# Attention with pooled keys and a gated layer on one core: exponentials by head from PSUM, and the order of POOL and w_out work

## Chip, cores and metric

The kernel runs on one core of one Trainium2 chip. The metric is the device time of one execution in microseconds (us). The kernel before took 963.73 us (median of 3 runs, 963.48 to 965.11).

## The reference

There are 8 batches of 8 heads, 576 positions and 64 numbers per head. Keys and values are averaged over groups of 8 positions, which leaves 72 of each. The attention result, 4608 rows of 512, goes through a gated layer with a hidden width of 1536.

```python
k_p = k.reshape(B, H, Sp, 8, D).mean(axis=3)
v_p = v.reshape(B, H, Sp, 8, D).mean(axis=3)
scores = scale * np.matmul(q, k_p.transpose(0, 1, 3, 2))
scores = scores - np.max(scores, axis=-1, keepdims=True)
attn = np.exp(scores)
attn = attn / (np.sum(attn, axis=-1, keepdims=True) + 1e-09)
x = np.matmul(attn, v_p)          # as rows: 4608 x 512
g = x @ w_gate
out = (g / (1.0 + np.exp(-g)) * (x @ w_val)) @ w_out
```

Each factor of the large products is carried as two 16-bit parts, a high and a low one, so one product of the reference is three matmuls.

## The kernel before, in words

**Tiles, pieces, steps.** The 4608 rows are cut into 9 tiles of 512. A tile is made of 4 or 5 *pieces* of up to 128 rows of one batch, 40 in all. `answer` takes a piece through the attention: scores on PE into two PSUM banks of four heads each (L578), `less_max` on DVE (per bank a maximum, L587, and a subtraction that also moves the scores to SBUF, L588), the exponent of all eight heads in one ACT instruction (L595 or L599), the row sums on DVE (L605 or L616), one or two small operations on the eight sums (L610 or L617) and their reciprocal (L611, L621). ACT and POOL then make the high and the low 16-bit part (L649, L654), a DMA transposes them, PE multiplies by the values (L678, L679), and DVE divides (L683). The first two batches (`b < SPLIT`, 10 pieces, called old) take an older route that normalises before the product (L625).

Each tile then takes 12 *steps*, one for each 128 columns of the hidden width. A *plain* step is 24 matmuls of 512 columns (`plain_step`, L775 to L777). A *fast* step saves a product: 7 products of 6 matmuls of 256 columns (`fast_step`, L879), between which ACT copies partial sums (L937, L939, L946) and DVE adds them (L942, L947). A fast step needs sums of the weights (`fast_weights`: DVE L800, POOL L806 and L819, ACT L812) and of the tile (`fast_x`: L840, L844, L845, L848), so a step is fast only from the time on when both stand. Tile 0 has 16 steps, some of half width; there are 112 steps, each with a tanh on ACT (L723) and two operations on DVE (L726, L731). The results go to memory, and the last stage, after the last step, multiplies them by w_out (L1586, L1600, L1601, operands from L1483, L1487, L1497).

**Beside the steps.** Batches 2 to 7 need pooled sums of keys and values: `kv_part` loads a sixth at a time and adds on POOL (L1169 to L1171). `out_weights` decodes the 64-bit w_out in 12 chunks, on DVE and ACT, and writes it back to memory.

**What sets the order.** `Order` (L64) writes the instructions of all engines in one order while the program is built. It keeps a planned time for each engine, takes the operation that could start first by its table of durations, and by rank among those that are close. Lines wait for flags (`yield flag(...)`), for buffers from pools (`get`, `put`), and a flag that is raised later moves work later. `tile_steps` makes a step fast when the weights' sums are planned to stand soon, and plain otherwise. On the chip every engine then works in this fixed order.

Of the kernel before, what the change touches and what calls it, by code (L numbers as in the profile page):

```python
# [9 lines left out]
F32 = mybir.dt.float32  # L10
# [4 lines left out]
ALU = mybir.AluOpType  # L15
# [48 lines left out]
class Order:  # L64
# [37 lines left out]
    def get(self, name):  # L102
        return "get", name

    def flag(self, name):
        return "flag", name
# [85 lines left out]
def attention_then_swiglu(  # L192
# [71 lines left out]
    nc.gpsimd.memset(shares[:, 1:2], 1.0 / POOLW)  # L264
    least = const.tile([P, 4], F32, name="least")
    nc.gpsimd.memset(least, 1e-30)
    logunit = const.tile([P, 1], F32, name="logunit")
    nc.gpsimd.memset(logunit, LOGUNIT)

    spare = early.tile([P, 2 * NJ * SP + 6 * NJ * P // 2], F32, name="spare", tag="early")  # L270
    ksum = [
# [306 lines left out]
                nc.tensor.matmul(o, qt[rows, j, :n], keys[rows, j], start=True, stop=True)  # L578
        return pss

    def less_max(b, n, pss, sc=None, groups=(0, 1)):
        sc = sc or buffer(at, [P, H, SP], F32, "sc")
        mx = small.tile([P, 2, GH], F32, name="mx")
        heads = "p (j g) s -> p g j s"
        for g in groups:
            pv = pss[g][:n, : GH * SP].rearrange("p (h s) -> p h s", h=GH)
            nc.vector.tensor_reduce(out=mx[:n, g], in_=pv, axis=AX.X, op=ALU.max)  # L587
            nc.vector.tensor_tensor(  # L588
                out=sc[:n].rearrange(heads, g=2)[:, g], in0=pv,
                in1=mx[:n, g].unsqueeze(2).broadcast_to([n, GH, SP]), op=ALU.subtract,  # L590
            )
        return sc

    def exponentials(n, sc):
        nc.scalar.activation(sc[:n], sc[:n], AF.Exp, scale=EXPSCALE)  # L595

    def weights(b, n, sc):

        nc.scalar.activation(  # L599
            sc[:n], sc[:n], AF.Exp, bias=logunit[:n], scale=EXPSCALE  # L600
        )

    def row_sums(n, sc):
        sm = small.tile([P, H], F32, name="sm")
        nc.vector.tensor_reduce(out=sm[:n], in_=sc[:n], axis=AX.X, op=ALU.add)  # L605
        return sm

    def one_over(n, sm):
        ri = small.tile([P, H], F32, name="ri", bufs=4)
        nc.vector.tensor_scalar_add(sm[:n], sm[:n], 1e-9 * UNIT)  # L610
        nc.vector.reciprocal(ri[:n], sm[:n])  # L611
        return ri

    def inverse_sums(n, sc):
        sm = small.tile([P, H], F32, name="sm")
        nc.vector.tensor_reduce(out=sm[:n], in_=sc[:n], axis=AX.X, op=ALU.add)  # L616
        nc.vector.tensor_scalar(  # L617
            out=sm[:n], in0=sm[:n], scalar1=1e-9, scalar2=1.0 / UNIT, op0=ALU.add, op1=ALU.mult
        )
        ri = small.tile([P, H], F32, name="ri", bufs=4)  # L620
        nc.vector.reciprocal(ri[:n], sm[:n])  # L621
        return ri

# [76 lines left out]
    def scales(bs, mt):  # L700

        top = p2s[:, bs[0], 2:3]
        if len(bs) > 1:
            top = small.tile([P, 1], F32, name="top")
            nc.vector.tensor_max(top, p2s[:, bs[0], 2:3], p2s[:, bs[1], 2:3])
        nc.vector.tensor_mul(mt[:, :2], shares, top.broadcast_to([P, 2]))
        nc.vector.tensor_mul(mt[:, 2:3], mt[:, 0:1], mt[:, 1:2])
        rm = small.tile([P, 1], F32, name="rm")
        nc.vector.reciprocal(rm, top)
        ratios = {}  # L710
        for old in (True, False):
            some = [b for b in bs if (b < SPLIT) == old]
            if not some:
                continue
            r = small.tile([P, len(some)], F32, name=f"r{len(some)}", bufs=8)
            nc.vector.tensor_mul(r, p2s[:, some[0] : some[-1] + 1, 2], rm.broadcast_to([P, len(some)]))
            if old:
                nc.vector.tensor_single_scalar(r, r, 1.0 / UNIT, ALU.mult)
            ratios |= {b: r[:, n : n + 1] for n, b in enumerate(some)}
        return ratios  # L720

# [413 lines left out]
    def out_weights():  # L1135

        yield flag("decoded")
        for c in range(NCH):
            n, t0 = yield get("mid")
            tag, tf = yield get("wf")  # L1140
            wf = const.tile([P, DM], F32, name="wf1", tag=tag, bufs=1)
            _, t1 = yield get("load")
            t = yield bulk(512, lambda: o_load(c, n, wf), t0, t1)
            o = "out", c
            th = yield op("DVE", 330, lambda: w_shift(o), t)
            ts = yield op("ACT", 1260, lambda: w_sign(o), th)
# [30 lines left out]
    def prep(b):  # L1177

        split = yield flag("boxes")
        if b > SPLIT + 1:  # L1180
            split = yield flag(("split", b - 2))
        box(0)
        box(1)
        t = 0
        for c in range(6):
            order.start(("kv", b + 0.1 * c), kv_part(b, c, split))
        for c in range(6):
            t = max(t, (yield flag(("kv", b, c))))
# [54 lines left out]
    def answer(t):  # L1243
# [17 lines left out]
            t0 = max(t0, t1)  # L1261
        tp = yield op("PE", 1200 if t["n"] < 12 else 900, lambda: ps.update(scores(b, s0, m, homes)), ta, t0)
        put("qt", t["qt"], tp)
        for g in range(2):
            tm = yield op("DVE", 910, lambda: less_max(b, m, ps, sc, (g,)), tp, ts)
            put("att", homes[g], tm)
        tp = tm
        order.done(("scored", t["n"]), tp)
        if old:
            tp = yield op("ACT", 690, lambda: exponentials(m, sc), tp)  # L1270

            def sums_inv():
                t["ri"] = inverse_sums(m, sc)

            tp = yield op("DVE", 1300, sums_inv, tp)
            if t["n"] in ON_POOL:
                tp = yield op("POOL", 1300, lambda: normalise(nc.gpsimd, m, sc, t["ri"]), tp)
            else:
                tp = yield op("DVE", 750, lambda: normalise(nc.vector, m, sc, t["ri"]), tp)
            h, th = yield get("half")  # L1280
            half = halves[h]
            tp = yield op("ACT", 910, lambda: soft_high(m, sc, half), tp, th)
            tp = yield op("POOL", 1950, lambda: soft_low(m, sc, half), tp)
            put("sc", s, tp)
        else:
            te = tp = yield op("ACT", 865, lambda: weights(b, m, sc), tp)
            h, th = yield get("half")
            half = halves[h]
            tp = yield op("ACT", 665, lambda: blocks_high(m, sc, half), tp, th)
            tp = yield op("POOL", 1500, lambda: blocks_low(m, sc, half), tp)  # L1290
# [6 lines left out]
        r = rate[i][b]  # L1297
        if not old:

            def ratios():  # L1300
                sm = row_sums(m, sc)
                t["ri"] = one_over(m, sm)

            te = max(tr, (yield op("DVE", 1200, ratios, te)))
        where, t0 = yield get("wv" if old else "att")
        ps = {}
        x = xs[i]
# [378 lines left out]
    def all_lines():  # L1686
# [28 lines left out]
        for b in range(SPLIT, B):  # L1715
            left_of["b", b] = 0
        for n, (i, *sub) in enumerate(ahead):
            t = {"n": n, "at": (i, *sub)}
            left_of["b", sub[1]] = left_of.get(("b", sub[1]), 0) + 1
            if i < 2:  # L1720
# [82 lines left out]
```

## Time and profile before

| | |
|---|---|
| median of three runs | 963.73 us |
| the profiled execution | 958.7 us |
| its span, first to last instruction | 956.9 us |
| PE, DVE, ACT, POOL busy | 895.9, 717.6, 468.9, 580.4 us |
| mean granted clock of PE | 0.982 of full speed |

All rows below come from the profiled execution. Its time lies 1.8 us over its span and 5.0 us under the median. PE's busy time is modelled: matmuls are pipelined, and a matmul that is shown with 0.38 us can start every 0.22 us.

### The profile page before, as it was taken

The numbers are of one execution on the slowest core, as the hardware profiler recorded it, in microseconds if no ns is written. First come the engines' busy times: TensorE is split into PE (matmuls) and PEld (weight loads), VectorE is DVE, ScalarE is ACT, GpSimd is POOL, SyncE is SP. The second block draws the span as 40 slices with busy tenths as digits, with TensorE's granted clock in tenths as the row PEclk, the third lists the DMA queues.
The fourth block names the chain that finished last, engine by engine and source line by source line (L and its number), as shares of the span: only waits on it lengthen the run. The fifth ranks groups of instructions, "written<-read, shape, count | busy, mean of one in ns | idle before, by whom it ended". The sixth has DMA issues, their size and how long they took to land. (4 is left out here: it accounts for less than half of the span.)

```text
span 956.9 us, 17399 instructions
## 1 busy us (share of the span) xinstructions
PE 895.9 (94%) x6636; PEld 629.2 (66%) x6658; DVE 717.6 (75%) x1087; ACT 468.9 (49%) x809; POOL 580.4 (61%) x502
## 2 busy tenths in 40 slices
PE   5788898998989889999999999999899899999998
PEld 5775354444656667888888888888655455555554
DVE  7889898698877798688877645467737769496781
ACT  5578553334245455566664544355624344444442
POOL 3534998989988898454523404022646578678692
PEclk9799899999999999999999999999999999999999
DMA  9947857848748556557572421135560440806301
GB/s 342 289 123 245 264 149 188 227 117 210 187 127 220 171 116 165 151 116 173 136 161 81 97 72 57 56 108 196 195 217 23 164 188 21 309 23 241 111 23 66
DMA packets 134419, 146.53 MB, mean 153 GB/s; under 512 B 81600, under 2 KB 102080, under 8 KB 132032
## 3 DMA queue, kind: packets, MB, share of 16 engines
q1 hardware_dynamic: 134336, 145.42, 51.7%
q8 instruction: 52, 0.85, 0.4%
q14 instruction: 31, 0.25, 0.1%
HBM read 86.51 MB, written 40.89 MB: 133 GB/s over the span
## 5 line engine op out<-in xcount | busy, mean ns | idle before, releaser
L1600 PE MATMUL ps<-low,wsh 128*128 128x512 bf16 x384 | 146.2, 381 | 5.7 <-DVE low L1487 4.1
L879 PEld LDWEIGHTS <-mixed 128*128 128x128 f16 x1332 | 129.2, 98 | 23.4 <-issue 5.6
L879 PEld LDWEIGHTS <-wgv_h 128*128 128x128 f16 x1184 | 114.3, 98 | 33.2 <-issue 15.1
L723 ACT ACTIVATE hf<-ps,un 128x512 f32<-128x512 f32 (+1 forms) x112 | 74.8, 669 | 102.7 <-PE ps L879 62.3
L879 PE MATMUL ps<-xc,mixed 128*128 128x256 f16 x888 | 118.2, 274 | 3.5 <-ACT ps L939 3.5
L726 DVE SCALAR_TENSOR_TENSOR hf<-hf,ps 128x512 f32<-128x512 f32 (+1 forms) x112 | 74.1, 663 | 57.4 <-ACT hf L723 57.0
L879 PE MATMUL ps<-xc,wgv_h 128*128 128x256 f16 x592 | 104.8, 273 | 9.3 <-DVE ps L947 7.7
L777 PE MATMUL ps<-x,wgv_l 128*128 128x512 f16 (+1 forms) x304 | 110.5, 364 | 2.6 <-DVE wgv_l L389 2.6
L775 PE MATMUL ps<-x,wgv_h 128*128 128x512 f16 (+1 forms) x304 | 110.7, 364 | 0.4 <-ACT wgv_h L384 0.4
L776 PE MATMUL ps<-x,wgv_h 128*128 128x512 f16 (+1 forms) x304 | 110.6, 364 | 0.0
L731 DVE SCALAR_TENSOR_TENSOR hf<-ps,un,hf 128x512 f32<-128x512 f32 (+1 forms) x112 | 81.2, 726 | 34.3 <-PE ps L879 27.6
L879 PE MATMUL ps<-x,wgv_h 128*128 128x256 f16 x592 | 103.6, 273 | 2.5 <-ACT rs L937 2.4
L879 PE MATMUL ps<-xc,wgv_l 128*128 128x256 f16 x296 | 80.9, 273 | 0.0
L879 PE MATMUL ps<-x,wgv_l 128*128 128x256 f16 x296 | 80.7, 273 | 0.0
L1487 POOL TENSOR_TENSOR low<-wgv_h,hs 128x1024 bf16<-128x1024 f32 x18 | 51.2, 2867 | 33.2 <-ACT hs L1483 33.2
L1600 PEld LDWEIGHTS <-wsh 128*128 128x128 bf16 x384 | 37.5, 98 | 51.0 <-issue 9.5
L844 POOL TENSOR_TENSOR fx<-fx 128x256 f32<-128x256 f32 x40 | 29.1, 727 | 59.0 <-DVE fx L840 56.6
L879 PEld LDWEIGHTS <-wgv_l 128*128 128x128 f16 x592 | 57.9, 98 | 6.9
L1487 POOL TENSOR_TENSOR low<-wgv_h,more 128x1024 bf16<-128x1024 f32 x16 | 47.2, 2972 | 24.3 <-ACT more L1483 24.3
L879 PE MATMUL ps<-x,mixed 128*128 128x256 f16 x444 | 60.6, 273 | 0.8 <-DVE ps L942 0.8
L1169 POOL TENSOR_TENSOR in<-in 128x576 f32<-128x576 f32 x36 | 55.4, 1540 | 7.8 <-DMA in<-kv_parts 5.7
L1601 PE MATMUL ps<-hs,wsl 128*128 128x512 bf16 x148 | 57.2, 387 | 0.0
(182 smaller groups left out, 2110.0 us busy)
## 6 DMA issues: line engine op xcount, KB each, us to landing
hd<-hf SPq DMA_DIRECT2D x104, 256.0 KB, 2.2
in<-kv_parts SPq DMA_DIRECT2D x36, 576.0 KB, 4.6
ws<-w_all SPq DMA_DIRECT2D x36, 512.0 KB, 5.1
wgv_h<-hd SPq DMA_DIRECT2D x9, 1536.0 KB, 6.7
wgv_l<-hd SPq DMA_DIRECT2D x9, 1536.0 KB, 8.7
out_t<-ob SPq DMA_DIRECT2D x36, 256.0 KB, 2.9
qt<-q_rows SPq DMA_DIRECT2D x32, 256.0 KB, 3.6
wd<-wf SPq DMA_DIRECT2D x12, 256.0 KB, 2.2
```

What stands on the lines that cost most here:

```text
L723: nc.scalar.activation(hf, gate, AF.Tanh, scale=un[:, c, 0:1])
L726: nc.vector.scalar_tensor_tensor(out=hf, in0=hf, scalar=1.0, in1=gate, op0=ALU.add, op1=ALU.mult)
L731: nc.vector.scalar_tensor_tensor(out=out, in0=val, scalar=un[:, c, 2:3], in1=hf, op0=ALU.mult, op1=ALU.mult)
L775: nc.tensor.matmul(o, wh, x["h"][:, j, a:e], start=(j == 0), stop=False)
L776: nc.tensor.matmul(o, wh, x["l"][:, j, a:e], start=False, stop=False)
L777: nc.tensor.matmul(o, wl, x["h"][:, j, a:e], start=False, stop=(j == NJ - 1))
L844: t1 = yield op(eng, cost[0], lambda: on.tensor_sub(o, a, b), t1)
L879: nc.tensor.matmul(o, a, b, start=begin and j + n == 0, stop=j == HJ - 1 and n == 2, skip_group_check=True,)
L1169: nc.gpsimd.tensor_add(a[:, :4], a[:, :4], a[:, 4:])
L1487: lambda: on.tensor_sub(low[:, 2 * n : 2 * n + 2], src[:, 2 * n : 2 * n + 2], rows[n].bitcast(F32)),
L1600: nc.tensor.matmul(o, top, where[1][:, c], start=False, stop=False, skip_group_check=True)
L1601: nc.tensor.matmul(o, lo, x_up, start=False, stop=c == HC - 1, skip_group_check=True)
```

## The change

The DVE no longer subtracts the maxima. It takes both maxima of a piece (`maxima`), and one small operation turns them into biases, -scale times the maximum plus a constant by batch (`biases`). ACT then takes the exponent straight from PSUM, head by head (`exponentials`: eight instructions of 72 columns instead of one of 576), with the maximum as bias and the row sum from the accumulator. DVE adds a constant from a tile to the sums, multiplies by another for the first two batches, and takes the reciprocal. The two PSUM banks of a piece are given back after the exponents and no longer after the subtractions. Two gates are added: a chunk of w_out is decoded only when a step of tile 4 to 7 is begun (`OUT_FROM`), and the pooled sums of a batch from the fifth on are begun only after the first piece of the batch before it has its scores and exponents (`KV_GATE`). With them, the table of durations is new in `answer`, and the order of all engines follows from it.

```diff
+OUT_FROM = 4
+KV_GATE = 0
-    logunit = const.tile([P, 1], F32, name="logunit")
-    nc.gpsimd.memset(logunit, LOGUNIT)
+    logs = const.tile([P, 2, 2, GH], F32, name="logs")
+    tiny = const.tile([P, 2, H], F32, name="tiny")
+    for i in range(2):
+        nc.gpsimd.memset(logs[:, i], i * LOGUNIT)
+        nc.gpsimd.memset(tiny[:, i], (1e-9, 1e-9 * UNIT)[i])
...
-            nc.vector.tensor_reduce(out=mx[:n, g], in_=pv, axis=AX.X, op=ALU.max)
-            nc.vector.tensor_tensor(
-                out=sc[:n].rearrange(heads, g=2)[:, g], in0=pv,
-                in1=mx[:n, g].unsqueeze(2).broadcast_to([n, GH, SP]), op=ALU.subtract,
+            nc.vector.tensor_reduce(out=mx[:n, g], in_=pv, axis=AX.X, op=ALU.max)
+        return mx
+
+    def biases(b, n, mx):
+        nc.vector.scalar_tensor_tensor(
+            out=mx[:n], in0=mx[:n], scalar=-EXPSCALE, in1=logs[:n, int(b >= SPLIT)], op0=ALU.mult, op1=ALU.add
+        )
+
+    def exponentials(n, pss, mx, sc, sm, g):
+
+        for j in range(NJ):
+            h = 2 * j + g
+            nc.scalar.activation(
+                sc[:n, h], pss[g][:n, j * SP : (j + 1) * SP], AF.Exp, bias=mx[:n, g, j : j + 1], scale=EXPSCALE,
+                accum_out=sm[:n, h : h + 1],
             )
...
-        nc.vector.tensor_scalar_add(sm[:n], sm[:n], 1e-9 * UNIT)
-        nc.vector.reciprocal(ri[:n], sm[:n])
...
-        nc.vector.tensor_reduce(out=sm[:n], in_=sc[:n], axis=AX.X, op=ALU.add)
-        nc.vector.tensor_scalar(
-            out=sm[:n], in0=sm[:n], scalar1=1e-9, scalar2=1.0 / UNIT, op0=ALU.add, op1=ALU.mult
-        )
+        nc.vector.tensor_add(sm[:n], sm[:n], tiny[:n, int(b >= SPLIT)])
+        if b < SPLIT:
+            nc.vector.tensor_mul(sm[:n], sm[:n], ones[:n, :H])
         nc.vector.reciprocal(ri[:n], sm[:n])
...
-                nc.vector.tensor_single_scalar(r, r, 1.0 / UNIT, ALU.mult)
+                nc.vector.tensor_mul(r, r, ones[:, : len(some)])
...
         for c in range(NCH):
+            yield flag(("taken", OUT_FROM + c // 3, c % 3 * 4))
             n, t0 = yield get("mid")
...
             split = yield flag(("split", b - 2))
+            yield flag(("scored", begin[b - 1] + KV_GATE))
...
+        tp = yield op("DVE", 1200, peaks, tp)
+        sm = small.tile([P, H], F32, name="sm", bufs=4)
         for g in range(2):
-            tm = yield op("DVE", 910, lambda: less_max(b, m, ps, sc, (g,)), tp, ts)
-            put("att", homes[g], tm)
+            tp = yield op("ACT", 1300, lambda: exponentials(m, ps, t["mx"], sc, sm, g), tp, ts)
+            put("att", homes[g], tp)
...
-            te = tp = yield op("ACT", 865, lambda: weights(b, m, sc), tp)
...
-            te = max(tr, (yield op("DVE", 1200, ratios, te)))
+            te = max(tr, (yield op("DVE", 450, ratios, te)))
```

What this moves is read from the instructions of each engine as they stand in the two programs. Lines of the changed program are some 5 to 10 lower. First, DVE in the steps of tile 2, before the change: `mx` are maxima, `sc` scores, `sm` row sums, `ri` reciprocals, `hf` the hidden rows, `fw` and `room` weights whose sums are made.

```order
L731 SCALAR_TENSOR_TENSOR hf<-ps,un,hf 128x512
L605 TENSOR_REDUCE sm<-sc 128x8
L610 TENSOR_SCALAR sm<-sm 128x8
L611 RECIPROCAL ri<-sm 128x8
L587 TENSOR_REDUCE mx<-ps 128x4
L588 TENSOR_TENSOR sc<-ps,mx 128x4x72
L726 SCALAR_TENSOR_TENSOR hf<-hf,ps 128x512
L587 TENSOR_REDUCE mx<-ps 128x4
L588 TENSOR_TENSOR sc<-ps,mx 128x4x72
L800 TENSOR_TENSOR room<-wgv_h,wgv_l 128x1024
```

The same place of DVE after the change:

```order
L590 TENSOR_REDUCE mx<-ps 128x4 x2
L594 SCALAR_TENSOR_TENSOR mx<-mx,logs 128x8
L609 TENSOR_TENSOR sm<-sm,tiny 64x8
L612 RECIPROCAL ri<-sm 64x8
L722 SCALAR_TENSOR_TENSOR hf<-ps,un,hf 128x512
L792 TENSOR_TENSOR room<-wgv_h,wgv_l 128x1024
L717 SCALAR_TENSOR_TENSOR hf<-hf,ps 128x512
L609 TENSOR_TENSOR sm<-sm,tiny 128x8
L612 RECIPROCAL ri<-sm 128x8
L674 SCALAR_TENSOR_TENSOR sc<-ps,r_1820,ri 64x512
```

The subtractions (L588) and the sums over 576 columns (L605) are gone; a small operation on `mx` and `logs` (L594) is new, and the operations on `hf` of the steps stand closer together.

Next, ACT among the first fast steps, before: `rs` and `ps<-ps` are the copies of a fast step, `xc` operands of a tile, `mixed` weights' sums.

```order
L937 COPY rs<-ps 128x256
L845 CAST xc<-fx 128x1024
L939 COPY ps<-ps 128x256
L599 ACTIVATE sc<-sc,logunit 128x576
L649 CAST half_136<-sc 128x8x72
L812 CAST mixed<-fw 128x768
L812 CAST wgv_h<-fw 128x256
L599 ACTIVATE sc<-sc,logunit 128x576
L723 ACTIVATE hf<-ps,un 128x512
L946 COPY ps<-ps 128x256
```

And after:

```order
L929 COPY rs<-ps 128x256
L602 ACTIVATE sc,sm<-ps,mx 128x72 x4
L931 COPY ps<-ps 128x256
L602 ACTIVATE sc,sm<-ps,mx 128x72 x4
L938 COPY ps<-ps 128x256
L714 ACTIVATE hf<-ps,un 128x512
L929 COPY rs<-ps 128x256
L640 CAST half_139<-sc 128x8x72
L804 CAST mixed<-fw 128x768
L804 CAST wgv_h<-fw 128x256
```

A piece's exponents are now two packs of four, and the copies of the fast steps (`rs`, `ps`) stand before, between and behind the packs, in a fixed order.

Last, POOL where the sums of weights for the fast steps begin (`fw`, `room`, `wgv_l`, `mixed`), before: `in` and `box<-in` are the pooled sums of keys and values, `half` the low parts of a piece.

```order
L806 TENSOR_TENSOR fw<-fw 128x256 x2
L1169 TENSOR_TENSOR in<-in 128x576
L1170 TENSOR_TENSOR in<-in 128x288
L1171 TENSOR_TENSOR box<-in 128x144
L654 TENSOR_TENSOR half_135<-sc,half_135 128x8x56
L655 TENSOR_TENSOR half_135<-sc,half_135 128x128
L806 TENSOR_TENSOR fw<-fw 128x256
L654 TENSOR_TENSOR half_136<-sc,half_136 128x8x56
L655 TENSOR_TENSOR half_136<-sc,half_136 128x128
L1169 TENSOR_TENSOR in<-in 128x576
L1170 TENSOR_TENSOR in<-in 128x288
L1171 TENSOR_TENSOR box<-in 128x144
```

And after:

```order
L798 TENSOR_TENSOR fw<-fw 128x256 x2
L1328 TENSOR_TENSOR box<-sc,box 128x512
L798 TENSOR_TENSOR fw<-fw 128x256 x2
L1328 TENSOR_TENSOR box<-sc,box 128x512
L811 TENSOR_TENSOR mixed<-fw,mixed 128x512
L811 TENSOR_TENSOR mixed<-fw,mixed 128x256
L811 TENSOR_TENSOR wgv_l<-fw,wgv_h 128x256
L798 TENSOR_TENSOR room<-room 128x256 x2
L645 TENSOR_TENSOR half_139<-sc,half_139 128x8x56
L646 TENSOR_TENSOR half_139<-sc,half_139 128x128
L798 TENSOR_TENSOR room<-room 128x256 x2
```

The pooled sums stood between the sums of weights; now none stands there. Counted over the whole of POOL's order, 2 of the 48 operations of L806 stand ahead of the fifteenth of the 36 groups of pooled sums before, and 30 stand ahead of the thirteenth now. Counted over PE's order, there are 74 fast steps before (3108 matmuls of L879, 42 to a step) and 81 now (3402), and 22 plain steps of tiles 1 to 8 before and 15 now. DVE joins a chunk of w_out after 18, 37, 39, 47 and on to 73 of the steps' operations L726 before, and after 51, 59, 63 and on to 95 now.

## Rows read from the trace of the kernel before

**Rows 1.** The page: busy time, share of span, instructions.
```profile
PE 895.9 (94%) x6636; PEld 629.2 (66%) x6658; DVE 717.6 (75%) x1087; ACT 468.9 (49%) x809; POOL 580.4 (61%) x502
```

**Rows 2.** Windows by tile: stretch, length, busy time (instructions) by engine, clock, DMA, GB/s.
```profile
0.00:140.00 140.00, 113.14 (x835) 81.74 (x836) 123.55 (x234) 89.97 (x168) 83.01 (x105) 0.91 0.75 237
140.00:227.00 87.00, 80.93 (x553) 41.47 (x550) 72.37 (x122) 32.60 (x53) 75.13 (x81) 0.98 0.67 174
227.00:303.00 76.00, 70.44 (x531) 43.11 (x530) 64.06 (x110) 33.17 (x57) 65.01 (x70) 1.00 0.76 193
303.00:381.00 78.00, 71.06 (x672) 55.43 (x671) 62.30 (x109) 38.40 (x74) 69.53 (x78) 0.98 0.59 154
381.00:447.00 66.00, 64.96 (x650) 56.36 (x649) 51.54 (x101) 42.00 (x82) 33.55 (x39) 1.00 0.59 142
447.00:512.00 65.00, 65.00 (x677) 56.54 (x676) 49.78 (x102) 37.08 (x72) 23.79 (x27) 1.00 0.62 147
```

**Rows 3.** Waits of PE from 140 to 450 us: in total, times, longest.
```profile
PE ps L879 <- DVE ps L947: 5.2, 6, 2.0
...
PE ps L879 <- ACT ps L939: 2.6, 2, 1.5
PE ps L879 <- ACT rs L937: 2.4, 2, 1.9
```

**Rows 4.** PE in time order inside a plain step: start, duration, instruction.
```profile
182.03 0.38 PE L777 MATMUL ps<-x,wgv_l 128*128 128x512 f16 x1
...
183.97 0.38 PE L777 MATMUL ps<-x,wgv_l 128*128 128x512 f16 x1
```

**Rows 5.** A window of fast steps alone, columns as in rows 2.
```profile
575.00:600.00 25.00, 25.00 (x230) 22.29 (x229) 13.25 (x24) 10.67 (x22) 10.33 (x12) 1.00 0.15 54
```

**Rows 6.** DVE groups: line, shapes, count, busy us, mean ns, idle before.
```profile
L588 DVE TENSOR_TENSOR sc<-ps,mx 128x288 f32<-128x288 f32 (+1 forms) x80 | 36.5, 456 | 7.9 <-POOL box L1333 3.1
...
L605 DVE TENSOR_REDUCE sm<-sc 128x8 f32<-128x576 f32 (+1 forms) x30 | 22.2, 740 | 0.0
...
L610 DVE TENSOR_SCALAR sm<-sm 128x8 f32<-128x8 f32 (+1 forms) x30 | 12.9, 431 | 1.0
...
L616 DVE TENSOR_REDUCE sm<-sc 128x8 f32<-128x576 f32 (+1 forms) x10 | 7.4, 742 | 0.3
```

**Rows 7.** A DVE group of 140 to 381 us alone, columns as in rows 6.
```profile
L610 DVE TENSOR_SCALAR sm<-sm 128x8 f32<-128x8 f32 (+1 forms) x17 | 8.6, 508 | 0.6
```

**Rows 8.** ACT groups by shape, columns as in rows 6.
```profile
L723 ACT ACTIVATE hf<-ps,un 128x512 f32<-128x512 f32 x104 | 71.1, 685 | 99.4 <-PE ps L879 62.3 <-PE ps L777 32.4 <-POOL box L1171 3.6
...
L599 ACT ACTIVATE sc<-sc,logunit 128x576 f32<-128x576 f32 x24 | 18.6, 774 | 23.7 <-DVE sc L588 23.3 <-DVE un L960 0.4
...
L723 ACT ACTIVATE hf<-ps,un 128x256 f32<-128x256 f32 x8 | 3.8, 471 | 3.3 <-PE ps L777 2.1 <-POOL un L1036 1.2
```

**Rows 9.** ACT in time order: two instructions with a row sum.
```profile
24.87 0.63 ACT L369 ACTIVATE wgv_h<-mixed 128x512 f16<-128x512 f32 x1 [3.10 <-DVE mixed L358]
25.41 0.19 ACT L369 ACTIVATION_READ_ACCUMULATOR wgv_h<-mixed 128x1 f32 x1
25.50 0.61 ACT L369 ACTIVATE wgv_h<-mixed 128x512 f16<-128x512 f32 x1
```

**Rows 10.** A small DVE operation by line: count, min/median/max ns.
```profile
L610 DVE TENSOR_SCALAR sm<-sm x30: 163/172/1621, 152.0 to 539.5; 128x8 f32<-128x8 f32 x24, 64x8 f32<-64x8 f32 x6
```

**Rows 11.** Another small one, of two tiles, columns as in rows 10.
```profile
L716 DVE TENSOR_TENSOR r<-p2s,rm x10: 158/695/1265, 27.2 to 516.4; 128x2 f32<-128x2 f32 x6, 128x1 f32<-128x1 f32 x4
```

**Rows 12.** DVE in time order, twice, where a small operation is long.
```profile
231.21 1.26 DVE L716 TENSOR_TENSOR r<-p2s,rm 128x2 f32<-128x2 f32 x1
...
345.30 1.62 DVE L610 TENSOR_SCALAR sm<-sm 64x8 f32<-64x8 f32 x1
```

**Rows 13.** POOL in time order at the same two places.
```profile
231.04 1.41 POOL L1169 TENSOR_TENSOR in<-in 128x576 f32<-128x576 f32 x1
...
344.63 2.26 POOL L848 TENSOR_TENSOR xc<-fx,xc 128x512 f16<-128x512 f32 x2
```

More of the change, by code (lines that the diff above doesn't have):

```diff
@@ L579, in scores, with maxima @@
         return pss
-    def less_max(b, n, pss, sc=None, groups=(0, 1)):
-        sc = sc or buffer(at, [P, H, SP], F32, "sc")
+    def maxima(n, pss):
         mx = small.tile([P, 2, GH], F32, name="mx")
-        heads = "p (j g) s -> p g j s"
-        for g in groups:
+        for g in range(2):
             pv = pss[g][:n, : GH * SP].rearrange("p (h s) -> p h s", h=GH)
             nc.vector.tensor_reduce(out=mx[:n, g], in_=pv, axis=AX.X, op=ALU.max)
-            nc.vector.tensor_tensor(
-                out=sc[:n].rearrange(heads, g=2)[:, g], in0=pv,
-                in1=mx[:n, g].unsqueeze(2).broadcast_to([n, GH, SP]), op=ALU.subtract,
-            )
-        return sc
@@ L594, in exponentials @@
[L594 to L600, printed above, removed]
-        )
-    def row_sums(n, sc):
-        sm = small.tile([P, H], F32, name="sm")
-        nc.vector.tensor_reduce(out=sm[:n], in_=sc[:n], axis=AX.X, op=ALU.add)
-        return sm
-    def one_over(n, sm):
-        ri = small.tile([P, H], F32, name="ri", bufs=4)
-        nc.vector.tensor_scalar_add(sm[:n], sm[:n], 1e-9 * UNIT)
-        nc.vector.reciprocal(ri[:n], sm[:n])
-        return ri
@@ L614, in inverse_sums @@
-    def inverse_sums(n, sc):
-        sm = small.tile([P, H], F32, name="sm")
-        nc.vector.tensor_reduce(out=sm[:n], in_=sc[:n], axis=AX.X, op=ALU.add)
-        nc.vector.tensor_scalar(
-            out=sm[:n], in0=sm[:n], scalar1=1e-9, scalar2=1.0 / UNIT, op0=ALU.add, op1=ALU.mult
-        )
-        ri = small.tile([P, H], F32, name="ri", bufs=4)
+        return mx
[3 more added lines that the diff above has]
+        )
@@ new lines, in exponentials, with one_over @@
+    def exponentials(n, pss, mx, sc, sm, g):
[4 more added lines that the diff above has]
+                accum_out=sm[:n, h : h + 1],
+            )
+    def one_over(b, n, sm):
+        ri = small.tile([P, H], F32, name="ri", bufs=4)
+        nc.vector.tensor_add(sm[:n], sm[:n], tiny[:n, int(b >= SPLIT)])
+        if b < SPLIT:
+            nc.vector.tensor_mul(sm[:n], sm[:n], ones[:n, :H])
@@ L744, in attention_then_swiglu @@
     xs = {}
+    begin = {}
     ahead = [(i, *sub) for i in range(len(tiles)) for sub in tiles[i][2]]
@@ L1263, in answer, with peaks, ratios @@
         put("qt", t["qt"], tp)
+        def peaks():
+            t["mx"] = maxima(m, ps)
+            biases(b, m, t["mx"])
+        tp = yield op("DVE", 1200, peaks, tp)
+        sm = small.tile([P, H], F32, name="sm", bufs=4)
         for g in range(2):
-            tm = yield op("DVE", 910, lambda: less_max(b, m, ps, sc, (g,)), tp, ts)
-            put("att", homes[g], tm)
-        tp = tm
+            tp = yield op("ACT", 1300, lambda: exponentials(m, ps, t["mx"], sc, sm, g), tp, ts)
+            put("att", homes[g], tp)
         order.done(("scored", t["n"]), tp)
+        def ratios():
+            t["ri"] = one_over(b, m, sm)
+        te = tp
         if old:
[L1270 to L1275, printed above, removed]
+            tp = yield op("DVE", 450, ratios, tp)
             if t["n"] in ON_POOL:
@@ L1298, in answer @@
         if not old:
-            def ratios():
-                sm = row_sums(m, sc)
-                t["ri"] = one_over(m, sm)
-            te = max(tr, (yield op("DVE", 1200, ratios, te)))
+            te = max(tr, (yield op("DVE", 450, ratios, te)))
         where, t0 = yield get("wv" if old else "att")
@@ L1717, in all_lines @@
         for n, (i, *sub) in enumerate(ahead):
+            begin.setdefault(sub[1], n)
             t = {"n": n, "at": (i, *sub)}
```

## The prediction

> **What bounds the kernel now.** I read the page's busy totals first, then windows by tile, then the waits of PE, then the groups of DVE, ACT and POOL that the change touches. PE is busy for 895.9 of 956.9 us [rows 1], so no change beside PE can give more than the 61 us that it idles, and only those idle times count that DVE, POOL or ACT cause. The windows end where the tanh of the last step of a tile ends. PE idles 26.9 us in tile 0 (140.00 less 113.14), 6.1, 5.6 and 6.9 us in tiles 1 to 3, 1.0 in tile 4, nothing in tile 5 [rows 2]. That is 46.5 of the 61 us, so the ground to be won lies before 450 us; the change has no part in the last stage. In tiles 1 to 3 (241 us) DVE is busy 72.4 + 64.1 + 62.3 = 198.8 us, 82%, and POOL 75.1 + 65.0 + 69.5 = 209.7 us, 87%, while ACT has 104.2 us, 43% [rows 2]. In tile 5 DVE is at 77% and POOL at 37%, and PE has no idle time. That is the pattern the forecast rests on: with two engines above 80%, work that PE waits for stands in line behind other work. The waits of PE in that stretch name it: 5.2 us for DVE's second addition of a fast step (L947), 5.0 us for ACT's copies (L939, L937) [rows 3].
>
> **The change, part by part.**
>
> *More fast steps.* Seven of 22 plain steps become fast, by the order of PE. A plain step's matmuls start 0.2156 us apart (182.03 to 183.97 is nine of them), 24 make 5.17 us [rows 4]. In a window of fast steps alone 230 matmuls run in 25 us, 42 make 4.57 us [rows 5]. Seven times 0.60 is 4.2 us, on PE, which sets the end there. It is lost only where the fast step's copies and additions come late.
>
> *DVE, big operations.* The subtractions go: 80 by 0.456 = 36.5 us. The row sums go: 22.2 + 7.4 = 29.6 us [rows 6]. Together 66.1 us. The maxima stay.
>
> *DVE, small operations.* One is new for each of the 40 pieces (biases), and 10 more for the old ones; those on the sums (L610, L617) are exchanged one for one. The trace has no such operation on `mx`, but L610 works on the same eight columns: 163 ns at least, 1621 at most, 431 as mean [rows 6, 10]. Bounds for the 50 are 8 and 81 us; I take the mean of L610, 21 us, since the new ones stand in the same stretch. What makes L610 long is POOL: the one that starts at 345.30 ends at 346.92, and the POOL pair that runs then ends at 346.89 [rows 12, 13]. An operation of two tiles does the same: L716 starts at 231.21 and ends at 232.47, POOL's L1169 at 232.45 [rows 12, 13], and its median is 695 ns [rows 11]. So taking the constant from a tile is worth nothing by these rows, and I cost that edit at zero, with bounds of minus and plus 40 x (0.431 - 0.163) = 11 us of DVE time. The Trainium skill (SBUF — State Buffer, "Who interferes with whom") states that a VectorE instruction with two SBUF inputs contends with a GpSimd instruction that reads SBUF, and whichever starts first holds the shared ports to its end. By that rule the exchange removes no wait and each of the biases is a new one; the trace agrees (L716 ends 0.02 us after POOL's).
>
> DVE so loses 66.1 - 21 = 45 us. In tiles 1 to 3 alone, 17 pieces take their sums [rows 7]: 17 x (0.912 + 0.740) = 28.1 us go and 17 by the local mean of 0.508 us come, 8.6 us: 19.5 us less of 198.8, and DVE's share falls from 82% to 74%, below that of tile 5.
>
> *ACT.* One exponent of 576 columns becomes eight of 72 from PSUM with a row sum. A tanh from PSUM with a scale from a tile takes 685 ns for 512 columns and 471 for 256 [rows 8], 0.836 ns a column, and 317 ns at 72. The instruction that reads the sum takes 0.19 us by itself, but the next starts 0.09 us after it (25.41, 25.50), and it starts 0.54 us after an instruction that takes 0.63 (24.87, 25.41) [rows 9]: a pair costs the duration of the first, to 0.01 us. So a pack of four takes 1.25 us, a piece 2.5 us. If the two did not overlap, it would be 8 x 0.51 = 4.1 us. The old exponent took 0.774 us, 0.68 of it before the next could start. I take 1.85 us more for a piece, 74 us in all (upper bound 136), on an engine that is busy 468.9 of 956.9 us [rows 1]. In tiles 1 to 3, 17 pieces make 31 us, and ACT goes from 43% to 56%. That hides it, as long as no pack stands in front of a copy that PE waits for; without that cover see the third rival.
>
> *POOL and w_out.* The pooled sums move past the sums of weights, and each wait for the first piece of the batch before holds up only its own six loads and additions, which stand behind it in every queue. A batch lasts five pieces, some 65 us [rows 2], and its six additions of some 3.2 us need 19 us. So the gate is free, and POOL falls from 87% where DVE and POOL meet. The work of w_out moves from tiles 1 to 5 to tiles 4 to 7, where DVE and ACT have room; its last chunk is joined some five steps before the end of tile 7, for which the last stage waits. I cost both at zero, bounds minus 3 and plus 3 us (half of the 6 us that tiles 1 and 2 each idle).
>
> *What PE gets back in tiles 1 to 4.* They idle 19.6 us [rows 2]. DVE at 74% and POOL freed, the line is shorter but not gone, and 10.2 us of waits remain with ACT's copies and L947 in part [rows 3]. Tile 5, with DVE at 77%, shows that all may go; ACT's packs speak against. I take half, 10 us, bounds 0 and 19.6.
>
> *Tile 0.* DVE is busy 123.55 of 140 us, ACT 89.97 [rows 2]. The ten old pieces take 10 x (0.912 + 0.742) = 16.5 us off DVE and put 8.6 us of small operations on (20 by L610's mean); ACT gets 18.5 us, and goes from 64% to 77%, among the decoding of weights that the first steps need. DVE's share falls from 88% to 83%. These nearly cancel: I take 1 us of gain, bounds 5 of gain (two thirds of DVE's 7.9) and 9 of loss (half of ACT's).
>
> *Sum.* 4.2 + 10 + 1 = 15.2 us. The profiled execution would go from 958.7 to 943.5 us, its span from 956.9 to 941.7. The median of the runs lies 5.0 us above the profiled one: 963.7 - 15.2 = 948.5 us.
>
> **Rivals.**
>
> 1. *DVE's relief is eaten at POOL's ports.* If the 50 new small operations took the longest time of L610, 1.62 us, they would cost 81 us against the 66.1 removed, and DVE would stand as full as before. What is left is the fast steps' 4.2 us: 959.5 us. For it: medians of 0.7 us for L716. Against it: POOL is itself relieved in that stretch, and half of L610 took 172 ns or less [rows 10, 11]. The Trainium skill's section cited above speaks for it: more operations with two inputs, more waits.
>
> 2. *All of PE's idle time in tiles 1 to 4 goes.* 4.2 + 19.6 + 5 in tile 0 = 28.8 us: 934.9 us. For it: tile 5 has none. Against it: fast steps stand closer together, with two engines in each.
>
> 3. *Slower: the packs hold the copies of the fast steps.* There are three copies in each of 81 steps, each followed by matmuls that need it, and 60 packs of 1.25 us among them, in a fixed order that was planned with 1.3 us a pack. If a pack takes longer than planned (0.51 us for each exponent, so 2.0) and every second one stands in front of a copy, PE loses 30 x 0.8 = 24 us: 948.5 + 24 = 972.5 us. It decides from 15.2/60 = 0.25 us for each pack on. For it: PE waits for ACT already now, 5.0 us [rows 3]. Against it: rows 9 show the overlap, and three banks let PE go on with another step.
>
> **How the numbers follow.** The forecast has 0.60, the first rival 0.16, the second 0.10, the third 0.14. The likeliest case by itself runs from 940 to 957 us. The range reaches down to 933, just past the second rival, and up to 964, between the first rival and the third; what is left out is the third and a part of the second. A measurement of this kernel tells some 0.2%, 1.9 us, from no change. Below 961.8 lie nearly all of the forecast, the second rival and most of the first: 0.79. Within 0.2%: the rest of the first, 0.07. Above: the third, 0.14.
>
> **What would show it.** The fast steps: 81 x 42 matmuls, 4.57 us each in tiles 5 to 8. DVE: no subtraction, busy some 45 us less; biases with a mean near 0.43 us and a maximum at the end of a POOL operation. ACT: exponents of 0.32 us, packs of 1.25 us, busy some 70 us more. PE's idle time in tiles 1 to 4 near 10 us, DVE below 76% there. The last stage as long as before. I am wrong if exponents start 0.4 us or more apart, if PE's waits for ACT's copies grow past 15 us, if tile 0 gets longer than 145 us, or if PE's idle time in tiles 1 to 4 stays near 20 us.

## The result, and the profile after

The changed kernel took 950.62 us (median of 4 runs, 949.76 to 952.98), the kernel before 963.61 us beside it; the ratio is 0.9875 (95% interval 0.9841 to 0.9909), 13.0 us less by the medians, 12.0 by the ratio. The prediction said 948.5 us, 15.2 less. A second set, with the kernel before beside it, gave a ratio of 0.9859 (0.9834 to 0.9884). The profiled execution took 952.98 us, with a span of 951.2.

The page after gives busy time, share and instructions of each engine, to be read against [rows 1]:

```profile
PE 898.0 (94%) x6784; PEld 644.0 (68%) x6784; DVE 671.0 (71%) x1031; ACT 542.5 (57%) x1430; POOL 574.4 (60%) x505
```

DVE lost 46.6 us (717.6 to 671.0), ACT got 73.6 (468.9 to 542.5). The windows by tile, cut again at the tanh of each tile's last step, answer to [rows 2]:

```profile
0.00:139.30 139.30, 113.06 (x821) 83.15 (x822) 112.37 (x222) 106.75 (x316) 82.66 (x110) 0.90 0.77 236
139.30:223.60 84.30, 79.40 (x507) 39.92 (x506) 63.35 (x103) 43.21 (x146) 70.28 (x79) 0.96 0.43 111
223.60:296.40 72.80, 70.79 (x671) 55.94 (x670) 58.26 (x104) 45.72 (x161) 52.75 (x61) 1.00 0.60 166
296.40:361.20 64.80, 64.11 (x637) 54.71 (x636) 40.68 (x86) 37.37 (x111) 39.37 (x45) 1.00 0.44 116
361.20:430.60 69.40, 67.03 (x683) 56.41 (x682) 48.35 (x97) 48.52 (x166) 49.56 (x55) 1.00 0.69 192
430.60:497.60 67.00, 64.04 (x634) 54.84 (x633) 44.85 (x91) 44.38 (x134) 41.86 (x44) 0.97 0.77 186
497.60:565.40 67.80, 66.90 (x698) 57.85 (x696) 45.49 (x92) 45.71 (x149) 25.76 (x28) 1.00 0.53 136
...
678.30:951.20 272.90, 263.14 (x1158) 144.35 (x1157) 184.27 (x115) 110.49 (x130) 180.39 (x61) 0.99 0.35 128
```

In tiles 1 to 4 PE idles 4.9, 2.0, 0.7 and 2.4 us, 10.0 together, where it was 19.6. Tile 3 is 13.8 us shorter than it was by the same cuts (78.6 us). Tiles 4, 5 and 6 are longer (by the same cuts they took 65.6, 65.7 and 60.6 us), and work has moved there: the exponents of 15 pieces stand in tiles 1 to 3 where 19 did, 6 and 5 in tiles 4 and 6 where 4 and 2 did, and 12 of the 36 groups of pooled sums stand in tiles 4 and 5, which had none. Tile 5 idles 3.0 us and had none. POOL falls from 89% to 61% in tile 3.

PE's waits of 139.3 to 450 us answer to [rows 3]:

```profile
PE ps L871 <- DVE ps L939: 4.2, 5, 2.1
PE ps L583 <- ACT sc L602: 1.8, 2, 1.0
...
PE ps L871 <- ACT ps L931: 0.9, 2, 0.4
```

The copies cost PE 0.9 us and no longer 5.0; the second addition (L939) costs nearly what it did; new is that scores (L583) wait for exponents (L602), which hold the two score banks. The exponents by group (columns as in rows 6):

```profile
L602 ACT ACTIVATE sc<-ps,mx 128x72 f32<-128x72 f32 (+1 forms) x320 | 98.0, 329 | 14.3 <-DVE mx L594 14.0
```

The new biases (L594) as a group, and then they and the addition on the sums (L609) with least, median and longest ns:

```profile
L594 DVE SCALAR_TENSOR_TENSOR mx<-mx,logs 128x8 f32<-128x8 f32 (+1 forms) x40 | 17.8, 445 | 1.5
...
L594 DVE SCALAR_TENSOR_TENSOR mx<-mx,logs x40: 157/282/1782, 10.0 to 546.9; 128x8 f32<-128x8 f32 x32, 64x8 f32<-64x8 f32 x8
...
L609 DVE TENSOR_TENSOR sm<-sm,tiny x40: 117/168/2137, 14.1 to 555.8; 128x8 f32<-128x8 f32 x32, 64x8 f32<-64x8 f32 x8
```

And one piece's exponents on ACT in order of time:

```profile
308.61 0.32 ACT L602 ACTIVATE sc<-ps,mx 128x72 f32<-128x72 f32 x1
308.83 0.19 ACT L602 ACTIVATION_READ_ACCUMULATOR sc<-ps,mx 128x1 f32 x1
308.92 0.31 ACT L602 ACTIVATE sc<-ps,mx 128x72 f32<-128x72 f32 x1
...
310.99 0.41 ACT L929 COPY rs<-ps 128x256 f32<-128x256 f32 x1
```

They start 0.30 us apart, and the copy of a fast step that stands behind them starts 2.38 us after the first.

### The profile page after: what moved, and what is told of

Same layout as the page of the kernel before. It is cut to its first block, busy times and chain, and to the rows that moved or that the text cites. A ratio compares the mean times of both kernels' runs of the same rounds, so it can differ in the third digit from the quotient of the medians.

```text
span 951.2 us, 18195 instructions
## 1 busy us (share of the span) xinstructions
PE 898.0 (94%) x6784; PEld 644.0 (68%) x6784; DVE 671.0 (71%) x1031; ACT 542.5 (57%) x1430; POOL 574.4 (60%) x505
## 5 line engine op out<-in xcount | busy, mean ns | idle before, releaser
L871 PEld LDWEIGHTS <-mixed 128*128 128x128 f16 x1458 | 140.9, 98 | 23.0 <-issue 4.6
L871 PEld LDWEIGHTS <-wgv_h 128*128 128x128 f16 x1296 | 125.7, 98 | 31.1 <-issue 12.8
L871 PE MATMUL ps<-xc,mixed 128*128 128x256 f16 x972 | 126.8, 273 | 1.7 <-ACT ps L931 1.7
L871 PE MATMUL ps<-xc,wgv_h 128*128 128x256 f16 x648 | 113.7, 272 | 8.8 <-DVE ps L939 8.0
L871 PE MATMUL ps<-x,wgv_h 128*128 128x256 f16 x648 | 114.1, 274 | 0.3
L602 ACT ACTIVATE sc<-ps,mx 128x72 f32<-128x72 f32 (+1 forms) x320 | 98.0, 329 | 14.3 <-DVE mx L594 14.0
L767 PE MATMUL ps<-x,wgv_h 128*128 128x512 f16 (+1 forms) x248 | 89.3, 360 | 0.9 <-ACT x L680 0.9
L768 PE MATMUL ps<-x,wgv_h 128*128 128x512 f16 (+1 forms) x248 | 89.2, 360 | 0.8 <-DVE x L684 0.8
L769 PE MATMUL ps<-x,wgv_l 128*128 128x512 f16 (+1 forms) x248 | 89.0, 359 | 0.0
L602 ACT ACTIVATION_READ_ACCUMULATOR sc<-ps,mx 128x1 f32 (+1 forms) x320 | 69.1, 216 | 0.0
L1328 POOL TENSOR_TENSOR box<-sc,box 128x512 f16<-128x512 f32 (+1 forms) x30 | 37.5, 1249 | 49.7 <-ACT box L1327 49.5
```

Source lines behind the costliest of these rows:

```text
L602: nc.scalar.activation(sc[:n, h], pss[g][:n, j * SP : (j + 1) * SP], AF.Exp, bias=mx[:n, g, j : j + 1], scale=EXPSCALE, accum_out=sm[:n, h ...
L767: nc.tensor.matmul(o, wh, x["h"][:, j, a:e], start=(j == 0), stop=False)
L768: nc.tensor.matmul(o, wh, x["l"][:, j, a:e], start=False, stop=False)
L769: nc.tensor.matmul(o, wl, x["h"][:, j, a:e], start=False, stop=(j == NJ - 1))
L871: nc.tensor.matmul(o, a, b, start=begin and j + n == 0, stop=j == HJ - 1 and n == 2, skip_group_check=True,)
```

## The experiments

Each was timed in five rounds against the kernel before on its chip; ratios carry 95% intervals. "Changed" is the changed kernel. The question is which part brings the 13 us: the prediction put it down to VectorE's relief by the new exponents (and to the fast steps), with "POOL freed" named beside it but given no price; the rival explanation is that the two gates, which the prediction cost at zero, do it. The texts name their theories by letters, a set at a time.

**Exponents without the gates.** Two lines are taken out:

```diff
-            yield flag(("taken", OUT_FROM + c // 3, c % 3 * 4))
...
-            yield flag(("scored", begin[b - 1] + KV_GATE))
```

> The exponents by head, the biases and the constants from tiles, without the two gates (75 fast steps in its order; 74 before, 81 with the whole change). Theory A, that of the prediction: the relief of VectorE gives PE's idle time back in tiles 1 to 4 by itself, and the gates give the fast steps: some 6 to 8 us below the kernel before. Theory B: nearly all the gain is the order on POOL (sums of keys and values moved out of the way of the weights' sums), VectorE's relief is worth nothing: 0 to 1 us below before. Theory C: nearly all is VectorE's relief: 10 us or more below before.

953.44 us, ratio 0.9923 (0.9898 to 0.9948), 7.4 us less. The exponents do bring something by themselves, about half of the gain.

**Gates without the exponents.** The kernel before, with these two lines and `begin`.

> The kernel before with the two gates alone, old exponents (79 fast steps). Theory A: five fast steps by 0.6 us and a little of idle time, 3 to 5 us below the kernel before. Theory B: 9 to 12 us below before, about as the whole change. Theory C: 3 us below before, the fast steps alone.

947.47 us, ratio 0.9856 (0.9829 to 0.9883), 13.9 us less. The whole gain is there with subtraction, one exponent of 576 columns and DVE's row sums as before.

**One gate at a time.** From the changed kernel, the first line above is taken out (no gate on w_out), or the second (none on the pooled sums).

> The changed kernel without the gate on w_out (80 fast steps). Theories A, B and C: within 2 us of the changed kernel, since the decoding of w_out is some 2.5 us of VectorE and 2 us of ACT for each of 12 chunks and neither is full; if the gate matters, 3 us or more above the changed kernel.

955.24 us, ratio 0.9932 (0.9910 to 0.9954): about 7 us above the changed kernel's 0.9859, against the expectation.

> The changed kernel without the gate on the pooled sums (74 fast steps, as before the change). Theory A: the seven fast steps are lost, 4.2 us, and 1 to 3 us of idle time come back: 5 to 7 us above the changed kernel. Theory B: nearly all the gain is lost, 10 to 13 us above. Theory C: the fast steps alone, 4 us above.

958.65 us, ratio 0.9967 (0.9949 to 0.9985): about 10 us above, as theory B had it. This kernel computes wrong numbers (a relative error of 0.053 against the reference), and why is not known; it is timed as an order of instructions and nothing more, so what it says of the gate is weaker than the rest. Beside the exponents each gate is worth more than the prediction's bound, and neither keeps the gain without the other: with one gate (0.9932, 0.9967) the kernel is no faster than with none (0.9923). One gate alone beside the old exponents was not timed.

What PE does in tiles 1 to 4 is one window of each kernel (columns as in rows 2). Before:

```profile
140.10:446.80 306.70, 287.08 (x2395) 196.08 (x2392) 250.03 (x439) 145.88 (x263) 243.12 (x265) 0.99 0.66 167
```

Changed:

```profile
139.30:430.60 291.30, 281.33 (x2493) 206.99 (x2492) 210.65 (x387) 174.82 (x582) 211.96 (x238) 0.99 0.54 145
```

Exponents without gates:

```profile
141.60:441.10 299.50, 287.67 (x2426) 199.17 (x2425) 224.09 (x397) 185.01 (x611) 236.90 (x261) 0.98 0.65 171
```

Gates without exponents:

```profile
142.00:430.80 288.80, 279.13 (x2461) 202.57 (x2458) 234.55 (x427) 138.19 (x261) 224.35 (x250) 1.00 0.58 154
```

No gate on w_out:

```profile
139.60:437.80 298.20, 281.65 (x2477) 205.24 (x2476) 219.02 (x401) 186.08 (x589) 213.96 (x237) 0.99 0.63 165
```

No gate on the pooled sums:

```profile
140.10:443.60 303.50, 287.74 (x2417) 196.58 (x2416) 220.64 (x387) 177.19 (x603) 236.97 (x263) 0.99 0.61 157
```

Before, PE idles 19.6 us in this stretch; in the five others it idles 10.0, 11.8, 9.7, 16.6 and 15.8 us. With the gates alone DVE is busy 81% of that stretch, as before, and PE idles less than with exponents alone, where DVE is at 75%: DVE's share does not tell PE's idle time. Fast steps are 81, 75, 79, 80 and 74, against 74. The prediction's own sum (0.60 us for each fast step more, and the idle time of tiles 1 to 4 that is gone) gives 13.8, 8.4, 12.9, 6.6 and 3.8 us; measured by the ratios of these sets (for changed, of its second set) were 13.6, 7.4, 13.9, 6.5 and 3.2, each to some 2.5 us.

The waits of PE that the gates alone end, from 140 to 450 us, are those for transposed pieces and for copies. Before, beside [rows 3]:

```profile
PE ps L673 <- DMA pt<-half: 3.3, 4, 1.4
```

With the gates alone (L882 is the fast step, L950 its second addition, L942 a copy):

```profile
PE ps L882 <- DVE ps L950: 6.1, 7, 1.2
PE ps L882 <- ACT ps L942: 1.7, 2, 1.2
...
PE ps L665 <- DMA pt<-half: 0.5, 1, 0.5
```

The second addition costs as much as before. Which gate ends which wait is not shown.

The sum over tiles 1 to 4 is not the whole account. Up to the end of tile 8, PE idles 49.4 us before, 40.4 with the exponents alone and 43.1 with the gates alone (the rows stand in this order):

```profile
0.00:685.50 685.50, 636.08 (x5500) 485.03 (x5501) 533.75 (x972) 358.30 (x679) 399.80 (x442) 0.98 0.59 163
```
```profile
0.00:679.50 679.50, 639.10 (x5518) 490.56 (x5519) 487.11 (x905) 427.32 (x1283) 397.35 (x445) 0.97 0.58 164
```
```profile
0.00:674.10 674.10, 630.97 (x5590) 492.08 (x5591) 534.60 (x982) 363.64 (x694) 397.29 (x442) 0.98 0.58 165
```

So over all tiles the exponents alone return more idle time than the gates alone, with four fast steps fewer (2.4 us), and yet their kernel takes 6 us more. What parts the two, as far as the profiles show it, is the granted clock, exponents alone first:

```profile
core 0: 951.6 us, clock 0.975
```
```profile
core 0: 945.5 us, clock 0.984
```

The granted clock is full or half, so the span times (1 - clock) estimates what the half clock costs: 23.8 and 15.1 us here; in the mean of all runs 21.9 and 15.9 us, and 21.1 in those of the kernel before. Some 5 of the 13.9 us of the gates alone are the clock by this estimate. With it and the idle time of tiles 0 to 8, the sum gives 8.8 us for the exponents alone, 14.5 for the gates alone, 13.0 for the changed kernel's second set, and 7.6 and 2.8 with one gate. Why the clock stays full longer with the gates alone is not shown.

**Halves of the exponents.** The same chip took the changed kernel again, and the two mixtures of routes, by a condition in `answer` ahead of `peaks`:

```diff
+        if old:                       # old_by_subtraction; "not old" in new_by_subtraction
+            ... less_max, one exponent, row sums on DVE
+        else:
+            ... peaks, exponentials by head
```

> The changed kernel as it is, to have it on the same chip as the three others. The gates alone ran at 0.986 of the kernel before. Theory A: exponents by head and gates relieve the same waits of PE, and with the gates in place the exponents cost some 3 us, since ACT gives the score banks back later: 0.988 of before, 3 us above the gates alone. Theory B: they are neutral and the 3 us are chance: 0.986.

948.98 us, ratio 0.9859 (0.9834 to 0.9884).

> The changed kernel with the ten old pieces (tile 0 and part of tile 1) on the route of before, subtraction and one exponent; the 30 others by head. Theory A: the cost sits with the later pieces, in tiles 1 and 2: as the changed kernel, within 1.5 us. Theory C: the cost sits in tile 0, where ACT decodes the weights and the exponents by head add 18 us to it: 3 us below the changed kernel.

949.44 us, ratio 0.9864 (0.9844 to 0.9884).

> The other half: the ten old pieces by head, the 30 others on the route of before, with both gates (79 fast steps). Theory A: as the gates alone, 3 us below the changed kernel. Theory C: as the changed kernel, or above it.

949.61 us, ratio 0.9852 (0.9829 to 0.9875). All three lie within 0.0012 of each other, and the gates alone (0.9856) among them. With the gates in place the exponents by head are worth nothing, in either half, and cost nothing that five rounds can tell (each ratio is known to some 2.4 us): the 3 us by which the medians of the first sets set the gates alone ahead of the change are not there in this set.

**The exponents' cover.**

```diff
-        for j in range(NJ):
+        for j in [j for j in range(NJ) for _ in range(2)]:
             h = 2 * j + g
```

> The changed kernel with each exponent taken twice, one after the other (the same values into the same places): a pack of four takes 2.4 us and no longer 1.2, in the same order. ACT gets 95 us more. If the packs stand in front of the fast steps' copies or hold the score banks that PE waits for (the third rival of the prediction, and theory A): 80 packs by 0.25 to 0.6 us, 20 to 50 us above the changed kernel. If ACT's idle time hides them: 0 to 5 us above.

1067.02 us, ratio 1.108 (1.1054 to 1.1107): 118 us above the changed kernel, more than twice the upper expectation. But the packs became longer than was meant:

```profile
320.33 0.33 ACT L602 ACTIVATE sc<-ps,mx 128x72 f32<-128x72 f32 x1
...
320.78 0.32 ACT L602 ACTIVATE sc<-ps,mx 128x72 f32<-128x72 f32 x1
...
321.09 0.31 ACT L602 ACTIVATE sc<-ps,mx 128x72 f32<-128x72 f32 x1
...
323.33 0.36 ACT L929 COPY rs<-ps 128x256 f32<-128x256 f32 x1
```

An exponent that is taken again starts 0.45 us after its first time, the next one 0.31 us after that, so a doubled pack takes 3.0 us and not 2.4. ACT is busy 670.2 us, 127 more than in the second profile of the changed kernel (543.3), and not 95 more: the 118 us are less than what ACT got. The waits of PE (total, times, longest):

```profile
PE ps L583 <- ACT sc L602: 38.3, 19, 5.6
PE ps L308 <- ACT sc L602: 28.5, 11, 7.7
PE ps L871 <- ACT ps L931: 20.6, 17, 2.8
```

Over all lines of this view PE's waits grow from 49 us, in the second profile of the changed kernel, to 129. Of these 80 us, 51 are waits for the score banks, also by the sums over rows (L308) that use the same banks; the copies of fast steps (L931, L929) come next with 25.

The same kernel, with a longer pack in the table of durations:

> Each exponent twice as in exponents_twice (0.949 of the clock, 118 us above the changed kernel), but the order of all engines is made with 2.5 us for a pack and no longer 1.3. Theory A: the 118 us come from an order that was written for packs of 1.3 us, in which everything on PE stands where the plan had the banks free; with the true duration planned, other work fills the time: 15 to 45 us above the changed kernel. Theory B: ACT itself is too full with 95 us more: 80 us or more above.

```diff
-            tp = yield op("ACT", 1300, lambda: exponentials(m, ps, t["mx"], sc, sm, g), tp, ts)
+            tp = yield op("ACT", 2500, lambda: exponentials(m, ps, t["mx"], sc, sm, g), tp, ts)
```

1024.06 us, ratio 1.0643 (1.0616 to 1.067): 43 us less than with the wrong plan and 73 us above the changed kernel, so neither expectation. A bit over a third went with the plan. The rest is not parted by these runs: the banks are held longer, ACT is fuller, and the plan of 2.5 us is itself short of the 3.0 us that a doubled pack takes.

**The small operations.**

```diff
-        nc.vector.tensor_add(sm[:n], sm[:n], tiny[:n, int(b >= SPLIT)])
-        if b < SPLIT:
-            nc.vector.tensor_mul(sm[:n], sm[:n], ones[:n, :H])
+        if b < SPLIT: nc.vector.tensor_scalar(sm, +1e-9, * 1/UNIT)
+        else: nc.vector.tensor_scalar_add(sm[:n], sm[:n], 1e-9 * UNIT)
...
-        mx = small.tile([P, 2, GH], F32, name="mx")
+        mx = pss[0][:, GH * SP : GH * SP + H].rearrange("p (g h) -> p g h", g=2)
```

The first part is `scalars`, the last `maxima_in_psum`.

> The changed kernel with the small operations on the sums written with immediate constants again, not with tiles (L609, L711 and their like); the order is the same. Theory A, that of the prediction: both forms wait for POOL alike, so no difference: within 1.5 us of the changed kernel, the operation's mean near 0.43 us as before. Rival: the tile form frees the engines of each other's waits, so that this kernel is 3 us or more slower and its operation longer.

950.60 us, ratio 0.9882 (0.9855 to 0.9908), the operation's mean 394 ns over the 40 pieces (425 and 402 ns with tiles, in the two profiles of the changed kernel): no difference. The form with one input from a tile and constants in the instruction waits alike, up to 2146 ns.

> The changed kernel with the eight maxima of a piece written into the unused end of a PSUM score bank, so that the biases have one input in SBUF and one in PSUM; the order is the same. Theory A: the biases' long times are waits for POOL, which an operation with a single SBUF input has not: its mean falls from 0.445 us to 0.20 or less and its maximum from 1.8 us to under 0.3. VectorE gets 10 us less, the time of the kernel 0 to 3 us less. Rival: the long times have another cause (the chain behind the maxima), and the mean stays over 0.35 us.

```profile
L595 DVE SCALAR_TENSOR_TENSOR mx<-ps,logs x40: 157/166/168, 10.1 to 548.1; 128x8 f32<-128x8 f32 x32, 64x8 f32<-64x8 f32 x8
```

The same operation on the same numbers, with one input in PSUM, never takes over 168 ns, where with both in SBUF it took up to 1782; 27 of the 40 begin while POOL works. In the profile after, all 22 biases of more than 250 ns end within 0.03 us of the end of a POOL operation that ran when they began. DVE as a whole is busy 4.8 us less (666.2), not the 10 expected. The kernel takes 952.75 us, ratio 0.9906 (0.9884 to 0.9928): not faster than the changed one.

The last takes all small operations away that it can: the maxima in PSUM as above, no constant added to the sums (so the sums are the exponents' alone), and shorter durations in the plan:

```diff
-        nc.vector.tensor_add(sm[:n], sm[:n], tiny[:n, int(b >= SPLIT)])
...
-        tp = yield op("DVE", 1200, peaks, tp)
+        tp = yield op("DVE", 1060, peaks, tp)
...
-            tp = yield op("ACT", 1300, ...)      # exponentials
+            tp = yield op("ACT", 1200, ...)
...
-            tp = yield op("DVE", 450, ratios, tp)
+            tp = yield op("DVE", 340, ratios, tp)
...
-            te = max(tr, (yield op("DVE", 450, ratios, te)))
+            te = max(tr, (yield op("DVE", 220, ratios, te)))
```

> The changed kernel with the maxima in PSUM, without the addition of 1e-9 to the row sums (which are 1 or more, so that in this number format it changes nothing), and with the order made for the durations that were measured (maxima and bias 1.06, pack 1.2, reciprocal 0.22 us); 79 fast steps. Theory A: VectorE is not what PE waits for once the gates are there, so 28 us less on it bring little, and two fast steps go: 3 us below to 2 us above the changed kernel. Rival: VectorE's small operations stand in the chain from scores to exponents that holds the banks, and taking 0.3 us off each piece brings 5 us or more.

949.99 us, ratio 0.9877 (0.9849 to 0.9905), as the changed kernel. Its tiles 1 to 4:

```profile
138.70:431.80 293.10, 283.87 (x2497) 204.92 (x2493) 204.00 (x369) 176.69 (x595) 229.39 (x259) 0.99 0.62 162
```

DVE at 70%, PE's idle time 9.2 us. Of the 28 us that were to come off DVE, 16 did (654.8 us busy), 6.6 of them in this stretch, and PE's longest waits there are still for the second addition of a fast step (L940):

```profile
PE ps L872 <- DVE ps L940: 4.1, 2, 3.5
```

So PE still waits for DVE, and yet 16 us less on it bring nothing that can be measured.

Leaving out the doubled exponents, the versions with both gates stand in five different orders and lie between 0.9852 and 0.9906; those with one gate or none, in three orders, lie between 0.9923 and 0.9967. So it is not one lucky order that brings the gain. No version of the twelve is faster than the changed kernel or the gates alone beyond the intervals.

## Why the prediction was right, and which step was not

1. *Fast steps*: 81 as counted; six of the seven come with the gates, for without them there are 75. The sum of steps and idle time in tiles 1 to 4 agrees for five kernels to about 1 us. For three others it does not: over their own windows, whose rows are not shown, `maxima_in_psum` would have 12.6 us and has 9.1, `scalars` 15.2 and 11.4, `old_by_subtraction` 9.7 and 13.1. With the idle time of tiles 0 to 8 and the clock, as estimated above, they come to 7.2, 11.4 and 11.1 us.
2. *DVE's durations*: 46.6 us less, 45 forecast; the biases 0.445 us as mean, 0.431 taken; that they wait for POOL is shown by `maxima_in_psum` and by where they end. That constants from tiles are worth nothing is shown by `scalars`.
3. *ACT*: 73.6 us more, 74 forecast; exponents 0.30 us apart, 0.31 forecast.
4. *Tile 0*: 139.3 us (140.7 in the second profile), 139 forecast. The last stage took 272.9 us, 1.5 more than before by the same cuts, where none was forecast.
5. *PE's idle time in tiles 1 to 4*: 9.6 us less, 10 forecast. But the cause that was given most weight for it is not needed, and that the number fits is luck. The step "the gate is free ... I cost both at zero" failed: the gates alone return 9.9 us of idle time there and five fast steps, with DVE's work as before in the whole (717.0 us), though 15.5 us of it leave this stretch. From the changed kernel, 6.6 us of idle time come back without the gate on w_out, and 5.8 without the one on the pooled sums. DVE's relief returns 7.8 us when it comes alone and nothing beside the gates. Both take work out of the same crowded stretch, and they do not add up; the prediction priced only one of them, and so came to the right sum.
6. *What was missed in size*, 2.2 us: tiles 5 to 8 idle 7.2 us in the profile after, 2.9 before by the same cuts. Work that left tiles 1 to 3 stands there now; that it causes this idle time is not shown. The prediction also bounds the gain by PE's idle time and has no term for the clock: by the estimate above the clock gives the changed kernel 3.4 us in its second set (18.2 us against 21.6 before), and in its first set, where its own part is 21.4 us, next to nothing if the kernel before ran there as in the other sets.
7. *The third rival* did not come, but its mechanism is real, and the place was wrong: not the copies first, the score banks. Packs that were 1.8 us longer cost 118/80 = 1.5 us each; in the changed kernel the chip kept the plan (1.3 us planned, 1.2 taken).
8. *Open*: the profiled execution of before lay 5.0 us under its median. Its clock was 0.982, where the runs of before beside the experiments had 0.978 in the mean, 4 us by the estimate above. Between the profiled executions the spans differ by 5.7 us, and by 9.4 for the second profile of the change (947.5), where the medians differ by 13.0. The clock makes up 4.7 us in the first pair (0.977 after, 0.982 before) and nothing in the second (0.982); some 3 us stay open.

## What to carry to other kernels

Where two parts of a change relieve the same stretch, each shows a gain alone and they do not add up; only undoing one while the other stays tells which is needed, and here two gates, a line each, did all that the change with its new softmax route did. A busy share near 80% named a crowded stretch here, not its cause: moving work to a later time brought the gain, and 47 us less on the busy engine added nothing to it. A sum of idle time should take in the stretch that the work is moved to, and the granted clock. In an order fixed at build time, an operation that held a PSUM bank longer than planned was paid for nearly in full (118 us for 127 us more of ACT), so the planned duration is worth measuring first, that of a test kernel too.

## What the runs showed of the hardware

A wait of PE may be paid for twice. In the profile after, PE idled 1.05 and 0.76 us before two groups of scores at 206 us:

```profile
206.52 0.44 PE L583 MATMUL ps<-box,qt 64*128 64x72 f32 x2 [1.05 <-ACT sc L602]
207.71 1.98 PE L583 MATMUL ps<-box,qt 64*128 64x72 f32 x14 [0.76 <-ACT sc L602]
```

Then the granted clock stood at half, 1.2 GHz, for 6.8 us; the windows are before, at and after that stretch. They show the order of the two and not that one causes the other:

```profile
205.00:207.60 2.60, 0.91 (x5) 0.29 (x2) 2.60 (x4) 2.60 (x18) 0.21 (x1) 1.00 0.00 0
207.60:214.40 6.80, 6.69 (x26) 3.54 (x27) 3.98 (x7) 4.35 (x21) 5.65 (x8) 0.50 0.51 140
214.40:223.60 9.20, 9.20 (x57) 4.36 (x56) 4.75 (x8) 3.48 (x6) 7.03 (x8) 1.00 0.58 148
```

The second profile of the same kernel has the same waits and a shorter stretch:

```profile
209.00:216.00 7.00, 6.84 (x33) 3.27 (x34) 4.46 (x8) 4.55 (x22) 5.72 (x8) 0.76 0.55 149
```

Over the whole span the time at half clock adds up to 44 us in the first (mean clock 0.977) and to 34 us in the second (0.982); their spans are 951.2 and 947.5 us. In `exponents_twice` the mean clock fell to 0.949. Of its 118 us, PE's idle time up to tile 8 accounts for some 80 (123.9 us against 44.0 in the second profile of the changed kernel); the span times (1 - clock) is 54 us against 17, an estimate of 37 us for the slower clock.
